# A longer count from a DMA's issue to its landing in the list that orders a Fourier-mixing and Mish kernel, and a later start of the last stage's weight sums

## The chip, the cores and the metric

The kernel runs on one core of a Trainium2 chip. The metric is device time in microseconds (us) of one execution, the median of several runs. Five instruction streams run side by side, each in its own order, and wait for each other through semaphores: PE (TensorE, matrix products into eight PSUM banks), DVE (VectorE, elementwise work), ACT (ScalarE, copies and activation functions), SP (SyncE, which here only issues DMAs) and POOL (GpSimd, which here issues the stores).

## The reference

`x` is 2048 tokens by 640 features, all in float32.

```python
g = sigmoid((x * gate_w).sum(-1))
a = einsum("sd,ed->se", x, dft_hid_re);  b = einsum("sd,ed->se", x, dft_hid_im)
A = einsum("ts,se->te", dft_seq_re, a) - einsum("ts,se->te", dft_seq_im, b)
h = einsum("sd,df->sf", x, w1) + b1                   # f = 1728
B = einsum("sf,fd->sd", h * tanh(softplus(h)), w2)    # Mish, then dense
return g * A + (1 - g) * B
```

## The kernel before

**Products.** A float32 product is made of three matmuls: each operand is split into a high part (an ACT copy to fp32r, `..h`) and a low part (a DVE subtraction, `..l`), and `mm3` multiplies high by high, low by high and high by low. Every matmul takes a 128x128 weight block and a 128x512 operand. All large products are further cut by Strassen-Winograd's scheme, so that DVE adds and subtracts blocks before and after them.

**Stages, in order of PE's time.** The sequence transform (`seq`, to about 444 us, in between some early parts of the dense layer), the hidden transform (`hid`, to 581 us), the first dense layer with Mish (`dense_first(0)` from 581 to 632 us and `dense_first(1)` from 632 us on, mixed from 670 us with the first products of the last stage), and the second dense layer (`fin`, from 689 us to the end). Results that don't fit on chip are stored to scratch in HBM and loaded again: `u` and `y` are the transforms' results, `early` and `five` are parts of the first dense layer that were multiplied earlier, `act` its results.

**What sets the order.** The program is first recorded as a graph of operations (`Graph.add`): each has an engine, a duration by a formula, and the values that it reads and writes. `Graph.run` then walks through a count of time of its own and appends, engine by engine, the operation that is wanted first among those whose inputs it counts as made and whose buffers it counts as free; the buffer that an operation gets is chosen at the same moment. The order of PE's products is fixed beforehand; only the buffers in their operands can change. On the chip each engine runs its list in that order and waits where something is not there. The pools are 18 tiles `f` of 128x512, 6 tiles `x` of 128x640 (which also serve as `f` where nothing wants them), the operand pairs `r` and `w`, and the eight banks `ps`.

A DMA takes part in that count at two places. `dma` gives it the duration `DELAY + size / RATE`, from which the time follows at which it is wanted; and `run` counts its result as landed, and its buffer as free, at

```python
dma = max(now + DELAY, dma) + op.moves
end = dma + 0.1
```

where `moves` is `size / RATE`, 0.72 us for 256 KB. All transfers on SP and POOL thus share one line of 364 GB/s.

**The last stage's weight sums.** `fin` needs sums and differences of rows of `w2`. `Stage.make(k, since)` (L439) makes them ahead of time for each of six `k`: two loads of 256 KB (`f<-in_w2`), four DVE operations on 128x256, and two stores by POOL (`wf<k>`, `wt<k>`), which `Stage.low` loads again in the last stage. `since` is the earliest moment, in the list's own count, at which the two loads may be appended; the DVE sums are wanted 12 us after that. On the chip nothing waits for `since`; it only acts through the order.

The names that the steps below touch: `to_sbuf` (a copy from a bank to an `f` or `x` tile), `done`/`plus` (a finished bank is copied or added to an `f` tile, and stored), and in `dense_first`

```python
copy(bk[f][0], load_of(FS, early[t1, f]))
times(bk[f][0], "s2", [(w[f][1], k) for k in range(2)], False, True)
```

where a stored part is loaded, copied by ACT to a bank, and added to by PE.

Of the kernel before, what the change touches and what calls it, by code (L numbers as in the profile page):

```python
# [25 lines left out]
NR, NFS, NX, NW = 10, 18, 6, 26  # L26
MM = 0.2267
HOP, PROMPT, LATER, AHEAD = 0.15, 2.0, 8.0, 5.0
DELAY = 2.2
RATE = 364e3  # L30
CALM, CALM_DMA, NEAR = 1.0, 3.0, 3.0
GATES = 60.0, 10.0
# [3 lines left out]
WITHIN = 12.0  # L36
LEAD, LAG = 2, 2
BEHIND = 9
MADE = 560.0, 6.0
ENDS = 5  # L40
LEND = 0.0
LOWS = {8: 70.0, 5: 0.0}
# [23 lines left out]
class Graph:  # L66
# [75 lines left out]
    def run(self, pools):  # L142
# [59 lines left out]
        while left:  # L202
            began = False
            for e, line in ready.items():
# [24 lines left out]
                if e in ("SP", "POOL"):  # L229
                    dma = max(now + DELAY, dma) + op.moves  # L230
                    end = dma + 0.1
# [45 lines left out]
def fnet_mish_gate(ctx: ExitStack, tc: tile.TileContext, xn, xt, c_re, c_im, wd_re, wd_im,  # L277
# [46 lines left out]
    def dma(queue, emit, r, w, size):  # L324
        op = G.add(queue, emit, r, w, DELAY + size / RATE, 0.605 if queue == "SP" else 1.0)
        op.moves = size / RATE
        return op
# [631 lines left out]
    def w1_rest(again=False):  # L959
        if W1C and not again:  # L960
            return
        W1C.clear()
        W1R.clear()
        W1C.append(Val(W))
        split(W1C[0], 0, load(X, w1a[FC - 1], cols=D), 0, D)
        g, w = load(X, w1b, cols=KD * FR), Val(W)
        W1R.append(w)
        ks = [(w, (k, 0)) for k in range(KD)]

        def cut(t, n):  # L970
            return t[:, :KD * n].rearrange("p (k f) -> p k f", k=KD)
        act(lambda: nc.scalar.activation(cut(w.t[0], P)[:, :, :FR], cut(g.t, FR), AF.Copy), whole(g), ks, KD * FR)
        dve(lambda: nc.vector.tensor_tensor(cut(w.t[0], P)[:, :, FR:], cut(g.t, FR), f32(cut(w.t[0], P)[:, :, :FR]),
                                            op=OP.subtract), whole(g) + ks, ks, KD * FR)
# [363 lines left out]
    for k in range(FP):  # L1338
        fin.make(k, MADE[0] + MADE[1] * k)
    w1_rest(True)  # L1340
# [64 lines left out]
```

## Time and profile before

| | |
|---|---|
| Device time, median of 3 runs | 858.42 us (855.13, 858.42, 858.47) |
| Profiled execution, device time | 855.2 us |
| Its span, first to last instruction | 853.0 us |
| PE busy | 843.6 us, 3703 matmuls |
| DVE, ACT, POOL busy | 746.2, 533.2, 121.4 us |
| DMA | 239.42 MB, mean 281 GB/s |

In the profile's rows a time is counted from the span's start, `ps`, `f`, `x`, `r`, `w` are the pools' tiles with their numbers left out, and `L388` is the line of the matmul, `L361` that of an ACT copy, `L352` that of a DVE operation on two tensors, `L333` and `L343` those that issue loads and stores. A matmul's row lasts about 0.39 us, but matmuls overlap: what counts on PE is the distance from one start to the next. The device time is 2.2 us more than the span.

### The profile page before, as it was taken

The numbers are of one execution on the slowest core, as the hardware profiler recorded it, in microseconds if no ns is written. First come the engines' busy times: TensorE is split into PE (matmuls) and PEld (weight loads), VectorE is DVE, ScalarE is ACT, GpSimd is POOL, SyncE is SP. The second block draws the span as 40 slices with busy tenths as digits, with TensorE's granted clock in tenths as the row PEclk, the third lists the DMA queues.
The fourth block names the chain that finished last, engine by engine and source line by source line (L and its number), as shares of the span: only waits on it lengthen the run. The fifth ranks groups of instructions, "written<-read, shape, count | busy, mean of one in ns | idle before, by whom it ended". The sixth has DMA issues, their size and how long they took to land.

```text
span 853.0 us, 12456 instructions
## 1 busy us (share of the span) xinstructions
PE 843.6 (99%) x3703; PEld 695.2 (82%) x3703; DVE 746.2 (87%) x1357; ACT 533.2 (63%) x982; POOL 121.4 (14%) x222
## 2 busy tenths in 40 slices
PE   9999999999999999999999999999999999999998
PEld 6888888877888788888888888887888888888886
DVE  7978889999998799989798999998585899899984
ACT  6966765657563754665587863744687877645442
POOL 0122110010100121121012102013421121011200
PEclk9999999999999999999999999999999999999999
DMA  9998676968854799999688986669987698969973
GB/s 333 344 341 281 218 255 202 378 212 292 297 173 148 251 343 374 313 383 391 220 286 323 339 270 225 222 208 370 403 261 266 221 352 290 291 191 292 300 229 134
DMA packets 119123, 239.42 MB, mean 281 GB/s; under 512 B 15232, under 2 KB 23168, under 8 KB 119056
## 3 DMA queue, kind: packets, MB, share of 16 engines
q1 hardware_dynamic: 101072, 182.32, 63.2%
q0 software_dynamic: 17840, 56.18, 18.5%
q8 instruction: 29, 0.48, 0.2%
q14 instruction: 38, 0.31, 0.1%
q10 hardware_dynamic: 144, 0.13, 0.0%
HBM read 179.77 MB, written 58.80 MB: 280 GB/s over the span
## 4 chain that ended last, share of the span: by engine, by line
PE 77%; issue 10%; DMA 5%; DVE 5%; POOL 1%; ACT 1%; SPq 0%; POOLq 0%; ACTq 0%; DVEq 0%
PE ps L388 77%; DVE f L352 1%; DMA u<-f 1%; DMA x<-in_xn_dram 1%; DMA y<-f 1%; DMA f<-in_c_im_dram 1%; POOL u L343 1%; DMA f<-in_c_re_dram 1%; DVE x L1243 0%; DMA act<-f 0%; DMA f<-in_w_dram 0%; ACT f L361 0%; DVE ps L352 0%; DVE r6l L383 0%; DVE x L352 0%
## 5 line engine op out<-in xcount | busy, mean ns | idle before, releaser
L352 DVE TENSOR_TENSOR f<-f,f 128x512 f32<-128x512 f32 (+2 forms) x321 | 205.5, 657 | 9.0 <-ACT f L847 2.1
L361 ACT ACTIVATE f<-ps 128x512 f32<-128x512 f32 x150 | 87.1, 595 | 42.3 <-PE ps L388 27.9
L352 DVE TENSOR_TENSOR f<-ps,f 128x512 f32<-128x512 f32 x102 | 68.1, 686 | 25.1 <-PE ps L388 17.1
L343 POOL DMA_DIRECT2D act<-f x50 | 27.1, 542 | 111.3 <-ACT f L847 91.3
L382 ACT ACTIVATE r1h<-f 128x512 fp32r<-128x512 f32 x39 | 24.5, 629 | 27.8 <-DVE f L352 14.9
L361 ACT ACTIVATE ps<-f 128x512 f32<-128x512 f32 x65 | 37.9, 592 | 5.7 <-DVE f L352 2.8
L343 POOL DMA_DIRECT2D u<-f x33 | 17.8, 542 | 161.3 <-DVE f L352 112.0
L352 DVE TENSOR_TENSOR x<-x,x 128x256 f32<-128x256 f32 (+3 forms) x77 | 33.5, 449 | 8.1 <-DMA x<-in_xn_dram 4.6
L382 ACT ACTIVATE r7h<-f 128x512 fp32r<-128x512 f32 x41 | 25.8, 630 | 20.2 <-PE ps L388 11.7
L382 ACT ACTIVATE r5h<-f 128x512 fp32r<-128x512 f32 x37 | 23.4, 631 | 22.9 <-DVE f L352 11.2
L382 ACT ACTIVATE r6h<-f 128x512 fp32r<-128x512 f32 x43 | 27.2, 632 | 16.3 <-PE ps L388 11.9
L382 ACT ACTIVATE r4h<-f 128x512 fp32r<-128x512 f32 x39 | 24.6, 630 | 17.9 <-PE ps L388 10.2
L382 ACT ACTIVATE r3h<-f 128x512 fp32r<-128x512 f32 x42 | 26.4, 629 | 14.9 <-PE ps L388 12.0
L847 ACT ACTIVATE f<-f,b1s 128x512 f32<-128x512 f32 x34 | 24.5, 720 | 17.3 <-DVE f L352 17.1
L383 DVE TENSOR_TENSOR r7l<-f,r7h 128x512 fp32r<-128x512 f32 x41 | 28.1, 686 | 7.8 <-ACT r7h L382 7.7
L382 ACT ACTIVATE r2h<-f 128x512 fp32r<-128x512 f32 x40 | 25.2, 631 | 14.8 <-DVE f L352 7.1
L382 ACT ACTIVATE r0h<-f 128x512 fp32r<-128x512 f32 x40 | 25.2, 629 | 12.5 <-PE ps L388 6.7
L383 DVE TENSOR_TENSOR r6l<-f,r6h 128x512 fp32r<-128x512 f32 x43 | 29.5, 685 | 3.6 <-ACT r6h L382 3.6
L383 DVE TENSOR_TENSOR r3l<-f,r3h 128x512 fp32r<-128x512 f32 x42 | 28.8, 685 | 4.3 <-ACT r3h L382 4.3
L382 ACT ACTIVATE r8h<-f 128x512 fp32r<-128x512 f32 x39 | 24.6, 630 | 10.3 <-PE ps L388 5.3
L383 DVE TENSOR_TENSOR r2l<-f,r2h 128x512 fp32r<-128x512 f32 x40 | 27.4, 686 | 4.0 <-ACT r2h L382 4.0
L382 ACT ACTIVATE r9h<-f 128x512 fp32r<-128x512 f32 x34 | 21.4, 628 | 15.2 <-PE ps L388 6.3
(2382 smaller groups left out, 2813.6 us busy)
## 6 DMA issues: line engine op xcount, KB each, us to landing
f<-in_c_im_dram SPq DMA_DIRECT2D x105, 256.0 KB, 4.6
f<-in_c_re_dram SPq DMA_DIRECT2D x103, 256.0 KB, 5.0
f<-act SPq DMA_DIRECT2D x77, 256.0 KB, 5.0
f<-u SPq DMA_DIRECT2D x60, 256.0 KB, 5.2
act<-f POOLq DMA_DIRECT2D x50, 256.0 KB, 5.2
f<-in_xt_dram SPq DMA_DIRECT2D x40, 256.0 KB, 5.1
u<-f POOLq DMA_DIRECT2D x33, 256.0 KB, 5.3
x<-in_xn_dram SPq DMA_DIRECT2D x24, 320.0 KB, 4.6
```

What stands on the lines that cost most here:

```text
L343: dma(queue, lambda: ISSUE[queue].dma_start(d.t, v.t[:rows]), whole(v), whole(d), rows * N * 4)
L352: dve(lambda: nc.vector.tensor_tensor(o.t[rows, x], a.t[rows, y], b.t[rows, z], op=op), whole(a, b), whole(o), n)
L361: act(lambda: nc.scalar.activation(o.t, a.t, AF.Copy, scale=scale), whole(a), whole(o))
L382: act(lambda: nc.scalar.activation(r.t[0][:, :N], src.t[:, :N], AF.Copy), whole(src), [(r, 0)])
L383: dve(lambda: nc.vector.tensor_tensor(r.t[1][:, :N], src.t[:, :N], f32(r.t[0][:, :N]), op=OP.subtract), whole(src) + [(r, 0)], [(r, 1)])
L388: G.add("PE", lambda: nc.tensor.matmul(bank.t, w.t[wn][:, k * P:k * P + P], x.t[xn_][:, :N], start, stop, skip_group_check=True), [(w, (k, ...
L847: act(lambda: nc.scalar.activation(o.t[rows], src.t[rows], AF.Mish, **more), whole(src, table) + whole(b1s) * bias, whole(o), more=0.1)
```

## The change

Two numbers of the list are other ones; no operation is added or removed.

```diff
-DELAY = 2.2
+DELAY = 3.3
...
-MADE = 560.0, 6.0
+MADE = 600.0, 6.0
```

`DELAY` goes into both places shown above: a 256 KB transfer counts as landed 4.12 us after its issue where it was 3.02 us, and is wanted 1.1 us earlier. `MADE` is the pair from which `since` is made (`MADE[0] + MADE[1] * k`): the six weight sums may be begun from 600, 606, ... 630 in the list's count in place of 560, 566, ... 590. Since the list is made step by step, nearly all rows after the first microseconds stand elsewhere or use other buffers. PE's products keep their order. Three places follow.

**ACT about 184 us, where the last part of the first `seq` problem ends and the half problem behind it begins.** The names are tiles with their numbers; `f3_96<-ps1_66` and `f3_96<-ps3_68` are copies of banks into the same tile. Before:

```order
L361 ACTIVATE f3_96<-ps1_66 128x512
L382 ACTIVATE r0h_73<-f17_110 128x512
L361 ACTIVATE ps2_67<-f5_98 128x512
L382 ACTIVATE r3h_79<-f2_95 128x512
L373 ACTIVATE w6h_129<-f15_108 128x256
L382 ACTIVATE r6h_85<-f4_97 128x512
L361 ACTIVATE f3_96<-ps3_68 128x512
L382 ACTIVATE r1h_75<-f12_105 128x512
L361 ACTIVATE x5_116<-ps5_70 128x512
```

After:

```order
L361 ACTIVATE x0_111<-ps1_66 128x512
L361 ACTIVATE ps4_69<-f16_109 128x512
L361 ACTIVATE x2_113<-ps2_67 128x512
L382 ACTIVATE r2h_77<-f12_105 128x512
L382 ACTIVATE r5h_83<-f17_110 128x512
L361 ACTIVATE f16_109<-ps7_72 128x512
L382 ACTIVATE r0h_73<-f9_102 128x512
L361 ACTIVATE f17_110<-ps6_71 128x512
L361 ACTIVATE ps1_66<-f0_93 128x512
L373 ACTIVATE w7h_131<-x3_114 128x256
L382 ACTIVATE r7h_87<-f6_99 128x512
L361 ACTIVATE x0_111<-ps3_68 128x512
```

The copy out of `ps3_68` had the tile of the copy six rows earlier, which POOL stores in between (`u3_0<-f3`); now it has `x0_111`, whose store (`u1_1<-x0`) stands three stores earlier on POOL's list. At the same seam of the next `seq` problem (282 us) the copy out of `ps0_65` had `f0_93`, stored just before it as `u7_0`, and now has an `x` tile whose last use lies more than a hundred matmuls earlier.

**ACT about 588 us, where `dense_first(0)` begins to add to stored parts.** `ps5_70<-f1_94` is the copy of the first `early` part into a bank before, `ps1_66<-f17_110` the same copy after. Before:

```order
L361 ACTIVATE ps2_67<-f6_99 128x512
L382 ACTIVATE r5h_83<-f4_97 128x512
L382 ACTIVATE w11h_139<-f9_102 128x512
L847 ACTIVATE f6_99<-ps7_72,b1s_169 128x512
L1008 ACTIVATE f16_109<-ps1_66 64x512
L361 ACTIVATE ps5_70<-f1_94 128x512
```

After:

```order
L361 ACTIVATE ps3_68<-f6_99 128x512
L382 ACTIVATE r7h_87<-f1_94 128x512
L361 ACTIVATE ps1_66<-f17_110 128x512
L361 ACTIVATE ps6_71<-f7_100 128x512
L373 ACTIVATE w1h_119<-x1_112 128x384
L382 ACTIVATE r9h_91<-f16_109 128x512
L847 ACTIVATE f7_100<-ps7_72,b1s_169 128x512
```

The copy moves ahead of the operands and of the first Mish (`L847`) that stood in front of it, and the weight sums that stood on DVE about there have gone to a later place.

**DVE, POOL and SP about 628 us, ahead of the seam from `dense_first(0)` to `dense_first(1)`.** On DVE, `f11_104<-ps6_71` is the last addition of a bank in `dense_first(0)`, and the three rows on 128x256 are weight sums of `k` = 2. After:

```order
L352 TENSOR_TENSOR f15_108<-f7_100,f13_106 128x256
L352 TENSOR_TENSOR f17_110<-ps1_66,f17_110 128x512
L352 TENSOR_TENSOR f13_106<-f13_106,f7_100 128x256
L352 TENSOR_TENSOR f12_105<-f16_109,f12_105 128x512
L352 TENSOR_TENSOR f11_104<-ps6_71,f11_104 128x512
L352 TENSOR_TENSOR f15_108<-f7_100,f15_108 128x256
```

The same tile `f15_108` is stored by POOL as `wt2` and then filled by SP with `early1_1`, which PE needs as the second stored part of `dense_first(1)`. SP after:

```order
L333 DMA f3_96<-five1_0_310 128x512
L333 DMA f7_100<-five1_1_311 128x512
L333 DMA f10_103<-early1_0_322 128x512
L333 DMA f14_107<-in_xt_dram 128x512
L333 DMA f15_108<-early1_1_323 128x512
L333 DMA f6_99<-in_xt_dram 128x512
L333 DMA f7_100<-in_w2_dram 128x512
```

SP before, at the same loads:

```order
L333 DMA f15_108<-five1_0_310 128x512
L333 DMA f0_93<-five1_1_311 128x512
L333 DMA f6_99<-early1_0_322 128x512
L333 DMA f9_102<-in_xt_dram 128x512
L333 DMA f10_103<-early1_1_323 128x512
L333 DMA f7_100<-in_xt_dram 128x512
```

Before, no weight sum stood here any more, and `early1_1` went to a tile that DVE had finished with well before.

## The prediction

> **What bounds the kernel now.** I read the page first: the span, the busy shares, the clock, and the chain that ended last.
>
> ```profile
> span 853.0 us, 12456 instructions
> PE 843.6 (99%) x3703; PEld 695.2 (82%) x3703; DVE 746.2 (87%) x1357; ACT 533.2 (63%) x982; POOL 121.4 (14%) x222
> PEclk9999999999999999999999999999999999999999
> PE 77%; issue 10%; DMA 5%; DVE 5%; POOL 1%; ACT 1%; SPq 0%; POOLq 0%; ACTq 0%; DVEq 0%
> ```
>
> PE is busy for 99% of the span at a clock of 0.9 or more throughout. It can't get better by more than its own waits, so these come next, from the view of waits of PE.
>
> ```profile
> PE ps L388 <- ACT f L361: 3.7, 2, 2.3
> PE ps L388 <- ACT ps L361: 0.6, 1, 0.6
> ```
>
> Two waits for a copy into an `f` tile and one for a copy into a bank; what PE waits beside that lies in the first five microseconds, whose rows stand alike in both lists. PE's timeline about the three:
>
> ```profile
> 190.03 0.39 PE L388 MATMUL ps<-r9l,w4h 128*128 128x512 f32 x1
> 190.26 0.39 PE L388 MATMUL ps<-r9h,w4l 128*128 128x512 f32 x1
> 192.94 0.50 PE L388 MATMUL ps<-r5h,w4h 128*128 128x512 f32 x1 [2.30 <-ACT f L361]
> 193.28 0.40 PE L388 MATMUL ps<-r5l,w4h 128*128 128x512 f32 x1
> ```
> ```profile
> 288.07 0.39 PE L388 MATMUL ps<-r9h,w4l 128*128 128x512 f32 x1
> 289.84 0.50 PE L388 MATMUL ps<-r5h,w4h 128*128 128x512 f32 x1 [1.38 <-ACT f L361]
> ```
> ```profile
> 587.83 0.39 PE L388 MATMUL ps<-w0h,w6l 128*128 128x512 f32 x1
> 588.80 0.50 PE L388 MATMUL ps<-r8h,w5h 128*128 128x512 f32 x1 [0.59 <-ACT ps L361]
> ```
>
> Undisturbed starts are 0.23 apart (190.03 to 190.26). So the waits cost 2.68 - 0.23 = 2.45, 1.77 - 0.23 = 1.54 and 0.97 - 0.23 = 0.74 us, and the first distance behind each is 0.34 (192.94 to 193.28), 0.11 more: 4.73 + 0.33 = **5.06 us**. That is all there is to gain: 0.6% of the span. What the copies waited for is in the chain that ended last:
>
> ```profile
> 187.50 4.69 DMA u<-f
> 192.29 0.61 ACT f L361
> ```
> ```profile
> 283.07 6.02 DMA u<-f
> ```
> ```profile
> 575.08 6.38 DMA y<-f
> ```
>
> Twice an ACT copy that frees a bank for PE waited until the store of its tile's last content had landed, 4.69 and 6.02 us after the issue. The third wait has the landing of a `y` store ahead of it, 6.38 us.
>
> **The first two waits: gained.** In the list a 256 KB store counted as landed after 3.02 us; it counts 4.12 us now. What the stores of `u` took over the whole run (median in the last column):
>
> ```profile
> u<-f POOLq DMA_DIRECT2D x33, 256.0 KB, 5.3
> ```
>
> And POOL's row for `u1_1` and the store behind it, from its timeline:
>
> ```profile
> 184.18 1.07 POOL L343 DMA_DIRECT2D u<-x  x2 [1.45 <-ACT x L361]
> ```
>
> A copy given the tile of a store 3 to 4 us old, as both of these were, therefore waits. In the new ACT list the first copy's tile comes from `u1_1`, three stores and three ACT copies earlier. It left at 184.18 before, 3.3 us ahead of `u3_0` at 187.50; with 5.3 us it lands at 189.5, and PE needs the copy (0.61 us) from 190.49 on, so begun at 189.85. Cover: 0.3 us at the median, nothing at a slow landing. The second copy's tile was last used more than a hundred matmuls earlier. I take both as gone: -2.45 - 1.54 - 0.22.
>
> The Trainium skill, page "DMA: Bandwidth & Descriptors", section on the anatomy of one DMA, fits a DMA as about 2.0 us plus its bytes at 436 GB/s; an estimate by it is 2.6 us for 256 KB. By that the old count of 3.02 was long enough and there is nothing to gain; the 5.3 us and the 4.69 us of the chain say otherwise, and the measured rows decide.
>
> **The third wait: gained here.** The weight sums leave this place. Before they stood in DVE's way directly:
>
> ```profile
> 580.17 1.29 DVE L352 TENSOR_TENSOR f<-ps,f 128x512 f32<-128x512 f32 x2 [0.83 <-DMA wt<-f]
> 581.37 0.42 DVE L352 TENSOR_TENSOR f<-f 128x256 f32<-128x256 f32 x1
> ```
>
> An addition out of a bank waited 0.83 us for a `wt` store to land, and sums of 0.42 us each (four for each `k`) stood among the operands that ACT then split. Both are gone, and the ACT copy stands ahead of the four operations that it followed (two operands, the first Mish, `L1008`): -0.74 - 0.11. What is late next there: the operand `r9h` behind the two copies, which in the new list has more rows between itself and its matmuls.
>
> **The weight sums at their new place: a new wait.** All that is moved: 12 loads on SP, 24 operations on DVE, 12 stores on POOL (POOL is 14% busy and SP only issues; neither queue is full). DVE's 24 x 0.42 = 10 us fall between 605 and 650 us, where PE follows DVE's bank additions closely (window 610 to 640: DVE, the fifth number, busy 22.32 of 30 us):
>
> ```profile
> 610.00:640.00 30.00, 30.00 (x134) 24.83 (x133) 22.32 (x37) 23.47 (x41) 7.55 (x14) 1.00 0.88 298
> ```
>
> There is room for them, but a sum that waits for its load would hold the addition behind it. From 590 to 612 us four of the six sums stood among such additions in the same way, and PE lost nothing: I cost them at nothing on DVE, with that as cover. The DMA engines pay. Two stretches of before, with and without weight sums (window 590 to 612 us, then 612 to 650):
>
> ```profile
> DMA packets 3899, 8.94 MB, mean 406 GB/s; under 512 B 560, under 2 KB 688, under 8 KB 3897
> f<-early SPq DMA_DIRECT2D x4, 256.0 KB, 6.2
> wt<-f POOLq DMA_DIRECT2D x4, 256.0 KB, 6.2
> ```
> ```profile
> DMA packets 4847, 10.78 MB, mean 284 GB/s; under 512 B 657, under 2 KB 657, under 8 KB 4843
> f<-early SPq DMA_DIRECT2D x6, 256.0 KB, 4.5
> ```
>
> A weight sum moves four times 256 KB, 1.05 MB. Four of the six now fall into the second stretch: (10.78 + 4.2) MB in 38 us are 394 GB/s, close to the 406 of the first. So landings there will be 6.2 us rather than 4.5.
>
> The place where it shows is `early1_1`, whose tile now has to be emptied by `wt2` first. Times of before for PE's side, the copy from its group:
>
> ```profile
> 628.62 0.68 DVE L352 TENSOR_TENSOR f<-ps,f 128x512 f32<-128x512 f32 x1
> ```
> ```profile
> 640.86 0.39 PE L388 MATMUL ps<-r8h,w22h 128*128 128x512 f32 x1
> ```
> ```profile
> L361 ACT ACTIVATE ps<-f 128x512 f32<-128x512 f32 x65 | 37.9, 592 | 5.7 <-DVE f L352 2.8 <-DMA f<-five 2.3 <-DMA f<-early 0.6
> ```
>
> The bank addition at 628.62 is tied to PE. Right behind it in the new list stands the sum: 629.30 + 0.42 = 629.7, the store `wt2` leaves at 629.75 and lands 6.2 later at 635.95; then the load leaves at 636.0 and lands at 642.2, the copy with its hand-over takes 0.7: 642.9. PE wants it at 640.86. So **2.0 us late**, and 0.11 for the start behind it. With the landings of the quieter stretch, 629.75 + 4.5 + 0.05 + 4.5 + 0.7 = 639.5: no wait at all. The upper end goes by the longest landing of all six `wt` stores:
>
> ```profile
> DMA to landing us min/median/max: 6.0/6.6/7.2
> ```
>
> 629.75 + 7.2 + 0.05 + 7.2 + 0.7 = 644.9, 4.0 us late. Ends 0 and 4.0, taken 2.0, because the traffic is nearest to the full stretch. Of the loads beside it `early1_0` has the least in hand: its tile is emptied by `act10_0`, and PE wants it six matmuls earlier.
>
> ```profile
> 625.56 0.54 POOL L343 DMA_DIRECT2D act<-f  x1 [5.60 <-ACT f L847]
> 639.50 0.39 PE L388 MATMUL ps<-r8h,w5h 128*128 128x512 f32 x1
> ```
>
> 625.6 + 6.2 + 0.05 + 6.2 + 0.7 = 638.7, 0.8 ahead of 639.5. The `in_xt` load behind `early1_1` on SP is held with it, and the wait at `early1_1` gives it the same time back.
>
> **Sum.** 853.0 - 5.06 + 2.0 + 0.11 = 850.05 us span; with the 2.2 us outside it, **852.2 us**. The profiled execution took 855.2 us. Two of the three other runs took 858.4, 3.3 us more. PE's starts are 0.23 apart everywhere but at its waits, so I take it that the 3.3 us arise in such waits, which go as well. That is an inference: no row of a single trace shows it.
>
> **Rivals.**
>
> *No gain from the longer count.* If the waits come back at other tiles, for instance at the first seam with its 0.3 us of cover, or if a 4.12 us count is still too short for landings of 5 to 6 us, the time stays between 855.2 and 858.4. For it: the count is still below the medians. Against it: the two tiles in question are 3.3 us and more than a hundred matmuls older than before, not 1.1 us. Chance 0.20, time 857. The page cited above would have it so, since by its 2.6 us no tile was given out too early.
>
> *DVE becomes the bound and gives the gain back.* The stretches of the first two waits and the one between them:
>
> ```profile
> 190.00:215.00 25.00, 22.70 (x100) 18.45 (x99) 24.24 (x47) 17.30 (x31) 0.00 (x0) 1.00 0.86 291
> 215.00:289.00 74.00, 73.45 (x325) 60.51 (x323) 64.02 (x104) 39.87 (x68) 7.55 (x14) 1.00 0.64 213
> 289.00:345.00 56.00, 55.16 (x243) 45.72 (x244) 54.90 (x91) 33.15 (x55) 9.69 (x18) 1.00 0.92 334
> ```
>
> DVE (the fifth number) worked 24.24 of 25 us and 54.90 of 56. Without 2.56 and 1.65 us of waiting PE needs 22.4 and 54.35, so the same DVE work there would be late by 1.8 and 0.55 us: 854.6. Against it: the stretch from 215 to 289 us has 10 us of DVE time to spare, and weights can be split ahead in it. Chance 0.13.
>
> *Slower: the chain store, load, copy at `early1_1` grows.* Each microsecond of landing costs twice there. The gain of 5.06 is used up when both landings take 7.7 us (15.4 + 630.5 - 640.86 = 5.0). The longest load of the run:
>
> ```profile
> DMA to landing us min/median/max: 2.3/4.9/9.3
> ```
>
> With 9.3 twice the wait is 8.2 us: 853.0 - 5.06 + 8.2 + 0.1 + 2.2 = 858.4, slower than the profiled execution by 0.4%. Chance 0.10. The Trainium skill, "TensorE: Matmul & The Clock Gate", section on the clock gate, adds that PE's clock is halved after an idle window of about 3.4 us; the clock rows here stay at 0.9 or more over a wait of 2.45, and no wait of this trace is long enough to show it.
>
> **Numbers.** My forecast has 0.57, with its own range 850.1 (no new wait) to 854.2 (4.0 late). The range over the cases runs from 849.8 (that low end less 0.3, since the costs are read from one execution) to 857.5, which leaves out the slowest fifth at most. 0.5% of 858.42 is 4.3 us, about what can be told from no change. Below 854.1 lie most of the forecast's cases (0.51) and a few of the DVE case: faster 0.54. Above 862.7 needs the slower case with still longer waits or one that I don't see: 0.06. The rest is 0.40.
>
> **What would show it.** Right: PE's waits have no rows about 190, 288 and 588 us; one row of 1 to 3 us stands near 635 us (PE on ACT `ps` L361, which waited for `f<-early`, behind `wt<-f`); the landings of 612 to 650 us have medians near 6. Wrong: `ACT f L361` rows again at the two seams, with `u<-f` behind them; or waits of PE on DVE between 190 and 345 us; or no wait near 635 and landings of 4.5. The sum is wrong as a whole if PE's starts are no longer 0.23 apart outside its waits.

## The result, and the profile after

The changed kernel takes **849.68 us** (median of 5 runs, 849.62 to 849.92). The kernel before took 856.28 beside it (5 runs, 854.88 to 858.47): a ratio of **0.9919, interval 0.9898 to 0.9940**. The forecast was 852.2, its range began at 849.8; the time lies 0.1 below it. Further sets on other chips stand among the experiments. Two executions on record, of 4901 and 1217 us where their neighbours took 850 to 860, are left out of every median and ratio.

The page after, the same lines as before:

```profile
span 847.6 us, 12444 instructions
PE 842.1 (99%) x3703; PEld 694.1 (82%) x3703; DVE 746.3 (88%) x1357; ACT 533.8 (63%) x982; POOL 122.0 (14%) x222
```

PE's waits after, from the view of waits:

```profile
PE ps L1221 <- PEq L1393: 0.8, 1, 0.8
PE ps L388 <- ACT ps L361: 0.3, 1, 0.3
PE ps L388 <- DVE r0h L380: 0.3, 1, 0.3
```

The 3.7 us on ACT `f` L361 are gone; one wait on ACT `ps` is left. ACT's copy at the first seam, PE's timeline there, and PE's timeline at the new wait:

```profile
188.45 1.28 ACT L361 ACTIVATE x<-ps 128x512 f32<-128x512 f32 x2 [1.41 <-PE ps L388]
```
```profile
189.38 0.39 PE L388 MATMUL ps<-r1h,w4l 128*128 128x512 f32 x1
189.61 0.39 PE L388 MATMUL ps<-r2h,w4h 128*128 128x512 f32 x1
```
```profile
634.85 0.39 PE L388 MATMUL ps<-r4h,w5l 128*128 128x512 f32 x1
635.56 0.50 PE L388 MATMUL ps<-r3h,w23h 128*128 128x512 f32 x1 [0.33 <-ACT ps L361]
635.90 0.39 PE L388 MATMUL ps<-r3l,w23h 128*128 128x512 f32 x1
```

The copy now waits for PE's result in its bank and no longer for a store. The pair of PE rows is the place of the 2.45 us wait (the matmul at 192.94 before): 0.23 apart now. The three rows at 635 us show the first product on `early1_1`: 0.71 - 0.23 = 0.48 us late, and 0.11 for the start behind it.

Adding up the distances between PE's starts that are over 0.227 us gives the whole balance of PE's row, whose last start moved from 848.51 to 843.12 us, by 5.39:

| | us |
|---|---|
| the three waits of before, with the starts behind them | -5.18 |
| a fourth small one of before (664 us) | -0.25 |
| the new wait at 635.6, with the starts behind it | +0.64 |
| small ones after (41, 70 and 347 us) | +0.54 |
| the first 10 us (first product 0.14 earlier, clock up sooner) | -1.17 |

The rows add up to -5.42; the rest is small change. Against the forecast span of 850.05 us, the 847.6 measured are 1.5 less by the new wait, 1.2 less by the start and 0.25 less by the wait at 664 us, and 0.5 more by the small ones. The last row is the start. PE's timeline of before, then of after:

```profile
4.57 1.62 PE L388 MATMUL ps<-r0h,w0h 128*128 128x512 f32 x3 [0.21 <-DVE r0h L380]
5.98 1.24 PE L388 MATMUL ps<-r0h,w0l 128*128 128x512 f32 x3
7.06 0.86 PE L388 MATMUL ps<-r0l,w0h 128*128 128x512 f32 x3
```
```profile
4.42 0.94 PE L388 MATMUL ps<-r0h,w0h 128*128 128x512 f32 x3 [0.31 <-DVE r0h L380]
5.20 0.85 PE L388 MATMUL ps<-r0h,w0l 128*128 128x512 f32 x3
```

Three products took 1.4 us before and 0.78 after: before, PE's clock rose only at 6.8 us, after at 3.7. (The trace after gives its granted clock as 0.95 from there on and the one before as 1.00; the undisturbed starts are 0.227 us apart in both, so no time is put down to that.)

### The profile page after: what moved, and what is told of

Read it like the earlier page. It is cut to its first block, busy times and chain, and to the rows that moved or that the text cites. A ratio compares the mean times of both kernels' runs of the same rounds, so it can differ in the third digit from the quotient of the medians.

```text
span 847.6 us, 12444 instructions
## 1 busy us (share of the span) xinstructions
PE 842.1 (99%) x3703; PEld 694.1 (82%) x3703; DVE 746.3 (88%) x1357; ACT 533.8 (63%) x982; POOL 122.0 (14%) x222
## 4 chain that ended last, share of the span: by engine, by line
PE 97%; DVE 2%; DMA 0%; issue 0%; ACT 0%; SPq 0%; DVEq 0%
PE ps L388 97%; DVE f L352 1%; DMA f<-in_c_im_dram 0%; DVE w10l L383 0%; DVE r4l L383 0%; DVE r3l L383 0%; DVE r1l L383 0%; DVE r2l L383 0%; ACT f L361 0%; DVE w13l L374 0%; DVE w12l L383 0%; ACT ps L361 0%; DVE r0h L380 0%; DVE x L705 0%; ACT x L703 0%
## 5 line engine op out<-in xcount | busy, mean ns | idle before, releaser
L352 DVE TENSOR_TENSOR f<-f,f 128x512 f32<-128x512 f32 (+2 forms) x314 | 202.7, 660 | 4.5 <-ACT f L847 3.3
L361 ACT ACTIVATE f<-ps 128x512 f32<-128x512 f32 x143 | 83.7, 596 | 40.6 <-PE ps L388 27.8
L352 DVE TENSOR_TENSOR f<-ps,f 128x512 f32<-128x512 f32 x96 | 64.1, 687 | 23.1 <-PE ps L388 20.2
L361 ACT ACTIVATE ps<-f 128x512 f32<-128x512 f32 x70 | 40.8, 595 | 8.6 <-DVE f L352 8.3
L382 ACT ACTIVATE r9h<-f 128x512 fp32r<-128x512 f32 x40 | 25.2, 631 | 28.4 <-DVE f L352 15.2
L847 ACT ACTIVATE f<-f,b1s 128x512 f32<-128x512 f32 x36 | 26.0, 722 | 21.4 <-DVE f L352 21.1
L382 ACT ACTIVATE r6h<-f 128x512 fp32r<-128x512 f32 x39 | 24.6, 631 | 18.5 <-PE ps L388 11.3
L382 ACT ACTIVATE r7h<-f 128x512 fp32r<-128x512 f32 x39 | 24.5, 627 | 15.6 <-PE ps L388 10.6
L383 DVE TENSOR_TENSOR r5l<-f,r5h 128x512 fp32r<-128x512 f32 x41 | 28.1, 687 | 5.9 <-ACT r5h L382 5.8
L382 ACT ACTIVATE r3h<-f 128x512 fp32r<-128x512 f32 x36 | 22.7, 630 | 16.1 <-PE ps L388 11.0
L343 POOL DMA_DIRECT2D u<-f x28 | 15.2, 544 | 122.1 <-DVE f L352 49.9
L383 DVE TENSOR_TENSOR r8l<-f,r8h 128x512 fp32r<-128x512 f32 x42 | 28.8, 686 | 1.2 <-ACT r8h L382 1.2
```

The costliest lines, as they stand in the source:

```text
L343: dma(queue, lambda: ISSUE[queue].dma_start(d.t, v.t[:rows]), whole(v), whole(d), rows * N * 4)
L352: dve(lambda: nc.vector.tensor_tensor(o.t[rows, x], a.t[rows, y], b.t[rows, z], op=op), whole(a, b), whole(o), n)
L361: act(lambda: nc.scalar.activation(o.t, a.t, AF.Copy, scale=scale), whole(a), whole(o))
L382: act(lambda: nc.scalar.activation(r.t[0][:, :N], src.t[:, :N], AF.Copy), whole(src), [(r, 0)])
L383: dve(lambda: nc.vector.tensor_tensor(r.t[1][:, :N], src.t[:, :N], f32(r.t[0][:, :N]), op=OP.subtract), whole(src) + [(r, 0)], [(r, 1)])
L847: act(lambda: nc.scalar.activation(o.t[rows], src.t[rows], AF.Mish, **more), whole(src, table) + whole(b1s) * bias, whole(o), more=0.1)
```

## The experiments

Three theories stood against each other. A: the count decides which tile a copy gets, and the waits were copies whose tile's store hadn't landed. B: the gain is the moved weight sums. C: part of it is the start, which differs between executions. All comparisons are with the kernel before on the same chip; its medians on the three chips were 856.98 (23 runs), 857.57 (21) and 858.30 us (6).

**The longer count alone.** `DELAY = 3.3`, `MADE = 560.0, 6.0`.

> The longer count alone (3.3), the weight sums as before (from 560). Theory A (the count decides which tile a copy gets): the waits of 2.45 and 1.54 us at the two seq seams are gone, as in the changed kernel; but with the sums still at 560 to 600 and every landing counted longer, the tiles for the first stored parts of dense_first(0) come late, so PE waits 1 to 3 us between 583 and 588 us instead of 0.74; device time 850 to 852.5. Rival B (the gain came from moving the weight sums): the seams' waits are back, device time 854 to 856. Rival C (1.2 us of the gain is only PE's clock rising sooner in one execution): the start of PE's row differs from execution to execution, in this kernel as in any, and device time scatters by about 1 us.

Measured: 853.74 (12 runs, 852.85 to 854.85), ratio 0.9960 (0.9942 to 0.9977). PE's timeline has the seams of `seq` undisturbed, and the rows with a wait are

```profile
582.81 0.50 PE L388 MATMUL ps<-w17h,w6h 128*128 128x512 f32 x1 [0.49 <-ACT ps L361]
585.04 0.50 PE L388 MATMUL ps<-r0h,w5h 128*128 128x512 f32 x1 [1.26 <-ACT ps L361]
```

Theory A by place, the time 1.2 us above its upper end. The count alone removes the `seq` waits and makes the one at the dense seam worse, from 0.74 to 2.1 us. In this trace 1.8 us of the span lie behind PE's last start, in the last output store: its issue on ACT's queue took 2.54 us, where it took 0.37 in the kernel before and the changed one. Whether the other eleven runs had that too isn't shown.

```profile
845.67 2.54 ACTq L710 DMA_DIRECT2D out_dram<-f  x1
```

**The later weight sums alone.** `DELAY = 2.2`, `MADE = 600.0, 6.0`.

> The later weight sums alone (from 600), the count as before (2.2). Theory A: up to 560 us the list is that of the kernel before, row for row, so both seam waits stand where they stood (2.5 and 1.5 us at about 190 and 288 us) and only the 0.74 us at 588 goes; nothing new near 635, since the list there has loads well ahead; device time 0.5 to 1 us below the kernel before, 854 to 857, and as scattered as that. Rival B: most of the gain, 850 to 851.

Measured: 855.78 (12 runs, 852.40 to 859.26), ratio 0.9990 (0.9964 to 1.0016). The waits of PE:

```profile
PE ps L388 <- ACT f L361: 2.2, 2, 1.2
PE ps L388 <- DVE ps L352: 1.6, 2, 1.4
```

The two `ACT f` waits are there again, and both copies waited for a `u<-f` store; the `DVE ps` waits lie at 158 us; the wait at 588 us is gone. B falls: by themselves the sums are worth nothing that 12 runs can tell. The two halves come to less than the whole (0.40% and 0.10%, together 0.8 to 0.95%). The traces show why: the later sums take away the 2.1 us at the dense seam that the longer count brings.

**Two more looks at the kernel before, unchanged.**

> The kernel before, unchanged, another look. Its executions lie 3.6 us apart, those of the changed kernel 0.3. Theory A: the scatter arises in the waits for stores' landings, so the two seam waits, 2.45 and 1.54 us in the first look, come out longer or shorter here, and the rest of PE's row is the same. Rival C: the scatter is PE's start (clock rising at 6.8 us in the one look and at 3.7 in the changed kernel's), and the seams are the same.

> The kernel before, unchanged, a third look. In the first two the waits were 2.5, 1.5 and 0.7 us (190, 288, 588 us) and 1.8, 1.1 and 2.1, with 1.5 us more at 158 us. Theory A: the same four places, other sizes; at least one of them over 1.5 us; everything else at 0.3 us or less; PE's clock rises between 3.5 and 7 us after the start.

Measured: 856.55 and 856.20 us. Some of PE's long waits, three rows of the first of these looks (`l1_before`), then four of the second (`l2_before`):

```profile
157.85 0.50 PE L388 MATMUL ps<-r1h,w7h 128*128 128x512 f32 x1 [0.94 <-DVE ps L352]
```
```profile
193.59 0.50 PE L388 MATMUL ps<-r5h,w4h 128*128 128x512 f32 x1 [1.60 <-ACT f L361]
```
```profile
590.32 0.50 PE L388 MATMUL ps<-r8h,w5h 128*128 128x512 f32 x1 [1.92 <-ACT ps L361]
```
```profile
190.42 0.39 PE L388 MATMUL ps<-r9h,w4l 128*128 128x512 f32 x1
193.40 0.80 PE L388 MATMUL ps<-r5h,w4h 128*128 128x512 f32 x1 [2.60 <-ACT f L361]
194.00 0.63 PE L388 MATMUL ps<-r5l,w4h 128*128 128x512 f32 x1
194.42 0.63 PE L388 MATMUL ps<-r5h,w4l 128*128 128x512 f32 x1
```

Same places, other sizes, in the order of the three traces of the kernel before: at 588 us 0.7, 2.1 and nothing over 0.3, at 190 us 2.5, 1.8 and 2.8, at 288 us 1.5, 1.1 and 1.5, at 158 us nothing, 1.5 and 0.7. So the scatter of the kernel before (853.46 to 862.63 over 23 runs) arises at least in part in these waits; the three looks took 855.2 to 856.6 us, and none of the longer executions was traced. In `l2_before` the wait of 2.8 us did more: the matmuls behind it start 0.43 apart. The windows ahead of, in and behind that stretch, with the granted clock as the last but two number:

```profile
185.00:190.00 5.00, 5.00 (x24) 4.14 (x23) 5.00 (x13) 4.19 (x9) 2.07 (x4) 1.00 0.71 219
193.00:196.00 3.00, 2.60 (x6) 2.12 (x7) 2.62 (x5) 3.00 (x7) 0.00 (x0) 0.50 1.05 374
197.00:200.00 3.00, 3.00 (x15) 2.47 (x14) 3.00 (x7) 2.86 (x6) 0.00 (x0) 1.00 0.91 300
```

Half the clock for 3.4 us, 1.5 us lost on top of the wait. The record has the mean granted clock of every run, and 0.998 for this one. Of the 50 runs of the kernel before on the three chips, the 18 with 0.999 or more took 853.46 to 857.04 us, the 32 with 0.998 or less 856.19 to 862.63. So lost clock is a second part of the scatter; where the untraced runs lost it, and behind which wait, isn't shown. C holds too, as something beside it: in thirteen traces the clock rose between 3.7 and 6.8 us (6.8, 4.9 and 5.1 for the kernel before, 3.7 and 6.0 for the changed one), and the first thirty products lost 0.1 to 1.2 us there.

**The count's two uses apart.** First the landings alone; in `dma`:

```diff
-op = G.add(queue, emit, r, w, DELAY + size / RATE, ...)
+op = G.add(queue, emit, r, w, 2.2 + size / RATE, ...)
```

> The changed kernel, but the 3.3 counts only where the list takes a transfer as landed and its tile as free; a transfer's own duration, from which follows how early it is wanted, has 2.2 again. Theory A (what counts is that no tile is given out before its store has landed): no wait at the two seq seams (the first seam's copy gets a tile that ACT and DVE have done with, the second's an x tile idle for 30 us); the loads of the dense seam are wanted later, so the wait near 636 us is longer than 0.6, about 1.3 us. Device time about 0.5 to 1.0 us above the changed kernel. Rival D (what counts is that loads are asked for earlier): the waits of 0.5 to 2 us come back at many places, 853 to 857.

Then the durations alone; in `run`:

```diff
-dma = max(now + DELAY, dma) + op.moves
+dma = max(now + 2.2, dma) + op.moves
```

> The other half: the 3.3 counts only in a transfer's duration, so that it is wanted 1.1 us earlier; landings count 2.2 again. Theory A: the second seam's copy has once more a tile stored 4.2 us before it, so 1 to 1.7 us of wait come back about 290 us, while at the first seam the tile happens to be one that DVE has done with; device time 1 to 3 us above the changed kernel and scattered over 2 us or more, like the kernel before. Rival D: as fast as the changed kernel and as steady.

Measured beside each other: landings alone 852.39 (5 runs, 850.76 to 854.21; 0.9940, 0.9915 to 0.9964), durations alone 856.46 (12 runs; 0.9988, 0.9970 to 1.0006), the changed kernel 849.60 (0.9905). The durations alone are worth nothing that 12 runs can tell: their trace has waits at both seams again.

```profile
194.28 0.50 PE L388 MATMUL ps<-r7h,w4h 128*128 128x512 f32 x1 [1.73 <-ACT f L361]
```
```profile
291.90 0.50 PE L388 MATMUL ps<-r9h,w4h 128*128 128x512 f32 x1 [2.10 <-ACT f L361]
```

The copies in front of them, the first from ACT's timeline, the second's store from the chain that ended last:

```profile
193.63 0.60 ACT L361 ACTIVATE f<-ps 128x512 f32<-128x512 f32 x1 [1.35 <-DVE r2l L383]
```
```profile
284.30 6.85 DMA u<-f
```

D falls. At the second seam the copy waited for its tile's store, as theory A says. That the first seam would be spared didn't come true: there the copy waited, by the profile, for `r2l`, a DVE operation, and not for a store. So not every late tile is one with a store under way. Of the landings alone the profile was of no use (an execution of 4901 us, whose matmuls start 1.28 us apart), so there was another look:

> The kernel with 3.3 in the landings alone, for its trace: it took 852.4 us where the changed kernel took 849.6. Theory A as stated: one wait of 1.3 to 2 us at the seam of the dense layer near 636 us and none at the seq seams. Theory F (loads that are wanted 1.1 us later leave ACT and DVE with inputs that land too late): several waits of 0.3 to 1 us on DVE at places where DVE is over 95% busy, 150 to 215 and 289 to 355 us, together 2 us or more.

851.06 us, and one wait of weight:

```profile
636.77 0.50 PE L388 MATMUL ps<-r4h,w5h 128*128 128x512 f32 x1 [1.07 <-ACT ps L361]
```

Theory A by place; the size, 1.24 us from start to start, is just under its 1.3, and the cause isn't the one that it names: the `early` load before it had landed at 634.82, and the copy began at 636.14, behind an operand and a Mish on ACT. F falls. Its trace explains 0.7 us beyond the changed kernel's wait; its runs on the other chip were 2.8 us slower, and this one execution lies at the fast end of theirs. So the earlier loads may be worth something beside the longer landings; the other 2 us stay open.

**The changed kernel once more,** beside the two halves of the count.

> The changed kernel once more, on the same chip as the three beside it: 849.0 to 851, waits only of 0.1 to 0.7 us, the longest at the seam of the dense layer near 635 us. The first five microseconds of PE's row show whether its clock again rises at 3.7 us (then the change has to do with it) or at another time between 3.5 and 7 us (then it hasn't).

Measured: 849.60 (6 runs, 849.13 to 850.02) against 857.57, a ratio of 0.9905 (0.9883 to 0.9928). Its one long wait is again

```profile
635.72 0.50 PE L388 MATMUL ps<-r3h,w23h 128*128 128x512 f32 x1 [0.35 <-ACT ps L361]
```

0.51 us late (0.74 behind the start at 634.98), and 0.11 behind it. The span is 847.7 us, although PE's clock rose only at 6.0 us here; so the early rise in the first trace is not needed for the gain, and with the same program rising at 3.7 and at 6.0 us the change doesn't set it.

**A still longer count.** `DELAY = 4.0`.

> The changed kernel with 4.0 in place of 3.3. If a longer count were only safer (the medians of landings are near 5), this is as fast as the changed kernel or faster. Theory A with its price: 18 f tiles and 6 x tiles that all count as taken 0.7 us longer run out where tiles turn over fastest, in the early parts of the dense layer from 79 to 96 us; the list itself has PE wait 0.5, 2.2, 1.5 and 1.9 us there, and the chip follows the list: 6 us of waits there, device time 853.5 to 857.

Measured: 853.55 (8 runs, 852.82 to 853.80), 0.9951 (0.9932 to 0.9969), with three waits of 1.37, 0.69 and 1.86 us, all in the early dense parts:

```profile
82.74 0.50 PE L388 MATMUL ps<-w20h,w16h 128*128 128x512 f32 x1 [1.20 <-ACT f L361]
88.37 0.50 PE L388 MATMUL ps<-r7h,w21h 128*128 128x512 f32 x1 [0.53 <-ACT f L361]
93.08 0.50 PE L388 MATMUL ps<-r0h,w24h 128*128 128x512 f32 x1 [1.70 <-ACT f L361]
```

The price of counting too long: tiles that are free on the chip count as taken, and the order made from that waits. From 68 to 90 us of this trace all transfers landed 3.0 to 4.6 us after their issue, where the list counts 4.72 for 256 KB. The place is right, the size 3.9 us in place of 6.

**What the wait at 635.6 us is.** In the changed kernel's trace, `wt2`'s store left about as forecast (10.6 us ahead of PE's need, 11.1 forecast), and everything behind it was quicker:

```profile
624.52 0.54 POOL L343 DMA_DIRECT2D wt<-f  x1 [0.99 <-DVE f L352]
```
```profile
628.70 1.87 SPq L333 DMA_DIRECT2D f<-early  x1
```
```profile
DMA to landing us min/median/max: 3.6/3.6/3.6
```
```profile
DMA to landing us min/median/max: 4.6/4.6/4.6
```

(the last two for this `wt` store and this `early` load). The load had landed at 633.33. ACT's timeline:

```profile
633.24 0.60 ACT L361 ACTIVATE f<-ps 128x512 f32<-128x512 f32 x1
633.90 0.63 ACT L382 ACTIVATE r9h<-f 128x512 fp32r<-128x512 f32 x1
634.44 0.58 ACT L361 ACTIVATE f<-ps 128x512 f32<-128x512 f32 x1
634.92 0.59 ACT L361 ACTIVATE ps<-f 128x512 f32<-128x512 f32 x1
```

The copy stood behind an operand and two evictions, 1.6 us after its data were there. To test that, the list may not append `r9h` and the short chunk's Mish before the copy. This kernel has two lines more, so its rows say `L390` for the matmul and `L363` for a copy:

```diff
+and (x[1] not in (5253, 5198) or 5240 in begun)
```

> The changed kernel, with one rule more for its list at the seam near 635 us: the operand r9h and the Mish of the short chunk may not be appended on ACT before the copy of early1_1 into its bank. Theory E (the 0.5 to 0.7 us at 635.6 are ACT's order: in the changed kernel's trace the load had landed at 633.33 and the copy began at 634.92, behind r9h, which waited for DVE): the copy begins at 634.3 to 634.6 and PE's wait there falls from 0.49 to 0.2 us or nothing; a wait of up to 0.4 may come 3 us later, at the products that need r9h or the late in_xt load. Theory P (as predicted: the landing of the load behind the wt2 store ended last): the copy begins no earlier and the wait stays at 0.5 us or more. Device time the same within its scatter, 849 to 850.

```profile
634.34 0.60 ACT L363 ACTIVATE ps<-f 128x512 f32<-128x512 f32 x1
```
```profile
634.72 0.39 PE L390 MATMUL ps<-r4h,w5l 128*128 128x512 f32 x1
634.99 0.50 PE L390 MATMUL ps<-r3h,w23h 128*128 128x512 f32 x1
```
```profile
637.91 0.50 PE L390 MATMUL ps<-w9h,w21h 128*128 128x512 f32 x1
638.64 0.49 PE L390 MATMUL ps<-w9l,w21h 128*128 128x512 f32 x1 [0.23 <-DVE w9l L385]
```
```profile
636.25 0.68 DVE L354 TENSOR_TENSOR f<-f,f 128x512 f32<-128x512 f32 x1
```
```profile
637.23 0.63 ACT L384 ACTIVATE w9h<-f 128x512 fp32r<-128x512 f32 x1
```

Theory E: the copy begins 0.6 us earlier, and the wait at it falls from 0.48 to 0.04 us. And 0.50 us come up 3 us later at the operand `w9`, so the time stays (850.07, 4 runs, 0.9909, 0.9891 to 0.9926). The load that this operand is made from wasn't late either: the `in_xt` load issued at 630.28 had landed at 634.25, the DVE sum began at 636.25 behind other DVE work, and the split at 637.23 behind a copy on ACT.

**The weight sums at other times.** `MADE = 620.0, 6.0`, then `580.0, 6.0`, both with 3.3:

> The changed kernel with the weight sums another 20 us later (from 620). The wait of 0.49 us at 635.6 us stands on the place of the sums among the loads, additions and copies ahead of the second half of the dense layer, so it goes if they are made past that seam: 0.6 us less than the changed kernel, about 849.1 (849.0 to 849.4). Rival: the sums only push the next seam's loads late, and a wait of the same size comes up behind it: 849.5 to 850.5.

> The changed kernel with the weight sums from 580 in place of 600. With 560 (and the count of 3.3) PE waited 0.65 and 1.43 us at 583 and 585 us, with 600 0.49 at 635.6, with 620 nowhere near either seam. If only the two seams of the dense layer matter, 580 lies between them and PE waits at neither: 849.0 to 849.5. If the sums' 6.3 MB in front of the first seam's loads are what matters, 580 still has two or three of the six there: 849.8 to 851.

From 620: 849.08 (6 runs, 848.23 to 850.20), 0.9915 (0.9895 to 0.9935); no wait at either dense seam, as expected, and 0.8 us near 348 us, which wasn't expected. From 580: **848.96** (4 runs, 848.54 to 849.08), 0.9894 (0.9878 to 0.9910); no wait of PE behind its start in the view of waits. It is the lowest median, but the intervals of 580, 600 and 620 overlap, so which of them is best isn't shown.

## Why the prediction was wrong, point by point

- **The three waits go.** Right: 5.06 forecast, 5.18 found, at the three places named; the two of `seq` by the count and the third by the moved sums, as the two halves show. The cover at the first seam was larger than the 0.3 us forecast from the whole run's median of 5.3: the two `u<-x` stores ahead of it landed 2.9 and 2.5 us after their issue, the later at 184.86, and the copy began at 188.45 and ended 0.56 us before PE's matmul.
- **A new wait at `early1_1`, 2.0 us.** This is the step that failed, right in its place and wrong in size and cause: 2.0 + 0.11 forecast, 0.48 + 0.11 found. The landings were 3.6 and 4.6 us, not 6.2 twice. The step behind it spread the sums' 4.2 MB evenly over 612 to 650 us. The chip moved 12.70 MB there, not 15, and moved them unevenly, 282 GB/s from 624 to 636 us and 403 from 636 to 650 (the last number), so the crowd came behind the seam:

```profile
624.00:636.00 12.00, 11.68 (x52) 9.38 (x51) 12.00 (x24) 9.90 (x19) 4.31 (x8) 0.95 0.85 282
636.00:650.00 14.00, 14.00 (x64) 11.54 (x62) 9.72 (x25) 9.92 (x19) 5.99 (x11) 0.95 1.04 403
```

The sign that the prediction set for the whole stretch, medians near 6 us, came true for most (`early` 6.9, `wt` 6.6, the `act` stores 5.8, `in_xt` only 4.2), and said nothing of the two transfers that counted. What ended last was ACT's order, as the run with the copy first shows.
- **The start taken as fixed.** No term of the sum had it, and the prediction read the clock as 0.9 or more throughout: 1.2 us of the 5.4 between the two profiled executions is the start, 1.0 of it PE's clock rising at 3.7 and not at 6.8 us. In the changed kernel's other trace it rose at 6.0, and the span was 847.7 nonetheless, since the small waits at 41 and 347 us were missing. So it doesn't carry the gain, but a range of single microseconds must hold it: the low end, 850.1 less 0.3, took over the start of one execution, the latest of the thirteen traced. That the time came out only 0.1 below that end is chance: against its case of no new wait, the new wait and the small ones added 1.2 us, and the start and the wait at 664 us took off 1.4.
- **The other runs' 3.3 us arise in waits that go as well.** Borne out as far as the spread shows: the changed kernel's runs lie within 0.3 us in the first set and 0.9 in the second (5 and 6 runs), those of before 3.6 and 7.7 apart (5 and 21). The lost clock belongs to it, and the prediction didn't have that.
- **The rivals.** No gain from the count: false, though the count alone holds half of it. DVE as the bound: 0.3 us at 347 us at most. The growing chain at `early1_1`: didn't come. By the fit of the Trainium skill, "DMA: Bandwidth & Descriptors", section on the anatomy of one DMA, an estimate for 256 KB is 2.6 us, and the change would have been worthless. The trace of before agrees for some stores (three of the `u<-x` stores from 184 to 187 us landed after 2.3 to 3.7 us), but those behind the two seam waits took 4.69 and 6.02, and they decided.

## What to carry to other kernels

This hand-made order lives on one figure for a transfer's landing, and of the three tried (2.2, 3.3 and 4.0 us, with the bytes' time on top) the middle one was best: too short, and copies get tiles whose stores are still under way, which costs little in one execution and more in another; too long, and tiles on hand count as taken. When such a figure is raised, look for the place where tiles or loads are now scarcest and move what can wait away from it: the count alone gave 0.4% here, the move alone nothing that could be told, both 0.8 to 0.95%. A wait on a copy that a load feeds is not a late load until the load's landing is compared with the copy's start.

## What the runs showed of the hardware

In one wait that made PE 2.8 us late (2.60 us idle by the profile) PE's clock fell to one half for 3.4 us; in one of 2.45 (2.30 idle) it did not. The Trainium skill, "TensorE: Matmul & The Clock Gate", section on the clock gate, puts this behind an idle window of about 3.4 us; the measured row says that less can be enough. The first rise of the clock came between 3.7 and 6.8 us after the start, and the first thirty products lost 0.1 to 1.2 us there, 0.7 to 0.8 us more in one execution than in another of the same program.
